# Attention, MLP and experts on one core: load order of the second batch, Silu on ScalarE, and where the early slots' token numbers are cast

## The chip, the core and the metric

One Trainium2 chip, one core of it. The time is that of one execution of the program on the device, in microseconds (us). Engines: TensorE (PE; its weight loads PEld), VectorE (DVE), ScalarE (ACT), GpSimd (POOL), and SyncE (SP), on whose queue nearly all loads and stores are issued, in order.

## The reference

Three stages, each on the output of the one before; the result is out, 2304 x 512.

```python
scores = scale * np.matmul(q, k.transpose(0, 1, 3, 2))          # 4 batches, 8 heads, 576 tokens, 64 wide
ret = np.matmul(scores * Dmat, v)                                # Dmat: causal, gamma[h] ** distance
x = ret.transpose(0, 2, 1, 3).reshape(B * S, H * D)              # 2304 x 512
h = x @ w_in                                                     # 512 -> 2048, w_in and w_out float64
x = ((h * (1.0 / (1.0 + np.exp(-h)))) @ w_out)                   # SiLU, 2048 -> 512
expert_idx = np.argmax(logits, axis=1)                           # logits: cosine of x and 8 expert rows, over tau
for e in range(8):
    mask = expert_idx == e
    out[mask] = gate_w[mask, None] * (np.maximum(x[mask] @ w1[e], 0.0) @ w2[e])
```

## The kernel before

**The MLP** is the frame of the first phase. The 2304 tokens are 6 blocks of 384, and a block takes 16 steps f, one for each 128 columns of w_in. A step has 12 matmuls into h (lines 829 to 831: x and w_in are each split into a high and a low part, xhi, xlo, winh, winl, and three of the four products are formed), then Sigmoid on ScalarE into sg (L834), the multiply of h and sg on VectorE (L835, recorded under the helper's line 137), the split of the result into gh (ScalarE, L843) and gl (POOL), and two steps later 9 matmuls into three y tiles (L857 to 859) with w_out's parts in wo. Steps are counted from 0 over all blocks.

**The weights** come as float64 while block 0 runs. Each of the 32 raw tiles (vraw, 512 KB; 16 of w_in in two DMAs each at L550, 16 of w_out at L547, in the order in which the steps use them) is turned into f32 by a pass on ScalarE (vg, L529) and three on VectorE (L533, L535, L537), then split by a cast on ScalarE (L591) and a subtraction on VectorE (winl or wo, L137). There are four raw buffers: a raw load goes when VectorE has made the last of the three passes on the raw four places earlier. KEPT w_out parts stay as wok; the others are stored in wod and read back as wr for the later blocks. Block 0's end is followed by ent, the expert rows (er), and by yr, the block's rows out of y.

**Attention** is spread under the steps. Batch 0 runs in the startup, batch 1's four head units under block 0, the tails of batches 0 and 1 (the last 192 tokens of each) under block 1, and so on. A head unit transposes q and k, forms three state products (L289), copies and sums them on VectorE (st, st, s: L313 and L137), masks the scores (pt), and in mix forms the rows of x (L264, L275), from which xhi and xlo of the next block are made. Batch 1's loads are 15 DMAs on SP, 256 KB for each third of v, k and q (vn L228, kn L237, qn L212); POOL scales vn and qn once they are in. The tails' kr and qr (L201) are loaded after the last raw; tails need transposes of them (kt, qt, L258).

**Order.** A scheduler places the instructions of each engine by its own model of their times; every engine then runs in that order, and waits for what is not there. issue_after(x) keeps an instruction behind x in the issue order. Batches 2 and 3 are loaded after `anchor`, a late reload of w_out; batch 1 is under no such rule.

**The router** scores the rows of a block against the 8 expert rows on VectorE (jv, L744), ranks the tokens of each expert (rp on TensorE, from oh) and scatters rows into slots (xs) and token numbers with gates into a table (tab). Experts 0 and 1 begin with their first 256 slots, while the last block's steps still run: early_jobs loads the table's part as tke (L974), casts the token numbers to tie (L977) and loads the slots' rows xr (L994). tie is used where an expert's output is scattered to out by POOL (L1150), in the second phase, in which each of the 8 experts goes through 8 steps of two layers; gl of a step is at L1128.

Of the kernel before, what the change touches and what calls it, by code (L numbers as in the profile page):

```python
# [12 lines left out]
AF = mybir.ActivationFunctionType  # L13
ALU = mybir.AluOpType
# [4 lines left out]
I32 = dt.int32  # L19
# [3 lines left out]
B, H, S, HD = 4, 8, 576, 64  # L23
NT, D, F1 = B * S, 512, 2048
E, F2 = 8, 1024
P = 128
KC = D // P
TB = 384
# [71 lines left out]
def body(tc, q, k, v, w_in, w_out, emb, tau, w1, w2, cst, out):  # L100
    nc = tc.nc
# [5 lines left out]
    sub = ALU.subtract  # L107
# [15 lines left out]
    cpool = pool("cpool")  # L123
# [12 lines left out]
    def tt(eng, o, a, b_, op):  # L136
        return eng.tensor_tensor(out=o, in0=a, in1=b_, op=op)  # L137

    def r2f(ap):
        return ap.bitcast(F32)  # L140
# [261 lines left out]
    def side_pv():  # L402
        return ps_v.tile([P, 512], F32, name="pv", tag="pv")

    def after_weights(on):
        return tc.issue_after(anchor[0].ins) if on else nullcontext()

    def prepare(u, psum):

        bt = u.bt  # L410
        if isinstance(u, HeadUnit):
            with after_weights(bt.b >= 2):
                if u.p % 2 == 0 and not bt.rows:
                    bt.load_rows(u.p, u.sg)
                if u.p == 0:
                    for c in range(3):
                        bt.load_chunk(c)
                        if bt.rows:
                            bt.load_queries(c)
            yield 0.05  # L420
        else:
            with tc.issue_after(rawload[0].ins):
                if u.p % 2 == 0:
                    bt.load_rows(u.p, u.sg)
                if u.p == 0:
                    for c in (3, 4):
                        bt.load_chunk(c)
            yield 0.05
        yield from u.prep(psum)
# [110 lines left out]
    def weights():  # L540
# [3 lines left out]
        def load(f, o):  # L544
            r = vpool.tile([P, D, 2], I32, name="vraw", tag="vraw", bufs=RAW)
            if o:
                rawload[0] = nc.sync.dma_start(r.rearrange("p d w -> p (d w)"), w_out32[P * f:P * f + P, :])  # L547
            else:
                for a in range(2):
                    nc.sync.dma_start(r[HD * a:HD * a + HD].rearrange("p (c f) w -> p c (f w)", c=KC),  # L550
                                      w_in32[256 * a:256 * a + 256, 2 * P * f:2 * P * f + 2 * P].rearrange("(c p) f -> p c f", p=HD))
            raw[f, o] = r


# [46 lines left out]
    l2done = [-1]  # L601
    anchor = [None]
    rawload = [None]
    wrload = [None]
    lastw = [None]

# [215 lines left out]
    def first_phase():  # L822
        gq = {}

        def l1(i, f):
            xh, xl = block_x(i)
            h = ps_h.tile([P, 512], F32, name="h", tag="h")
            for c in range(KC):
                nc.tensor.matmul(h[:, :TB], winh[f][:, c], xh[:, c], start=(c == 0), stop=False)  # L829
                nc.tensor.matmul(h[:, :TB], winh[f][:, c], xl[:, c], start=False, stop=False)  # L830
                nc.tensor.matmul(h[:, :TB], winl[f][:, c], xh[:, c], start=False, stop=(c == KC - 1))  # L831
                hook((c + 1) / 8)
            sg = gpool.tile([P, TB], F32, name="sg", tag="sg", bufs=2)
            nc.scalar.activation(sg, h[:, :TB], AF.Sigmoid)  # L834
            tt(nc.vector, sg, h[:, :TB], sg, ALU.mult)  # L835
            return sg

        last = [None]
# [126 lines left out]
    class Slots:  # L965


        def __init__(self, e0, e1, s0, n, m, nm):
            ne = e1 - e0
            self.e0, self.n, self.s0, self.m = e0, n, s0, m  # L970
            rows = tabv[e0:e1, s0:s0 + m]
            self.w = w = m // n
            self.tk = cpool.tile([P, ne, n, 2], F32, name=f"tk{nm}")
            load = nc.sync.dma_start(self.tk[:w].rearrange("p e i c -> p e (i c)"), rows.rearrange("e (p i) c -> p e (i c)", i=n))  # L974
            after_scatters(load, scatters)
            self.ti = cpool.tile([P, ne, n], I32, name=f"ti{nm}")
            nc.vector.tensor_copy(self.ti[:w], self.tk[:w, :, :, 0])  # L977

    class Job:

# [40 lines left out]
        nc.sync.dma_start(jb.raw[n][1], w2[e, n * w:(n + 1) * w].rearrange("(g p) d -> p g d", p=P))  # L1021

    early = []
    ep_ = []
    wp_ = [None]

# [27 lines left out]
    def second_phase():  # L1054
# [57 lines left out]
        def layer1(s):  # L1112
# [12 lines left out]
            gh = gpool.tile([P, TB], F32R, name="gh", tag="gh", bufs=LAG + 1)  # L1125
            gl = gpool.tile([P, TB], F32R, name="gl", tag="gl", bufs=LAG + 1)
            nc.scalar.activation(gh[:, :w], h[:, :w], AF.Relu)  # L1127
            nc.vector.scalar_tensor_tensor(out=gl[:, :w], in0=h[:, :w], scalar=0.0, in1=r2f(gh[:, :w]), op0=ALU.max, op1=sub)  # L1128
            return gh, gl

        def layer2(ss):
# [6 lines left out]
            for j in range(jb.n):  # L1138
# [7 lines left out]
                if f == NF2 - 1:  # L1146
                    e = jb.e - ts.e0
                    ob = gpool.tile([P, D], F32, name="ob", tag="yr", bufs=3)[:ts.w]
                    nc.scalar.activation(ob, y, AF.Copy, scale=ts.tk[:ts.w, e, i, 1:2])  # L1149
                    w = nc.gpsimd.indirect_dma_start(out=out, out_offset=bass.IndirectOffsetOnAxis(ap=ts.ti[:ts.w, e, i:i + 1], axis=0),  # L1150
                                                     in_=ob, in_offset=None, bounds_check=NT - 1, oob_is_err=False)
                    for w0 in puts:
                        tc.declare_no_dep(w.ins, w0.ins.name, reason="no two slots have a token in common")
                    puts.append(w)
# [110 lines left out]
```

## Time and profile before

| | us |
|---|---|
| median of 3 runs | 847.79 |
| lowest, highest | 844.42, 849.81 |
| the profiled execution | 848.8 |
| its span | 847.0 |
| TensorE busy in the span | 798.2 |
| VectorE busy | 538.9 |
| ScalarE busy | 364.9 |
| POOL busy | 263.9 |
| TensorE's idle time for the state sum s, one wait | 5.1 |
| VectorE's idle time for the table tke, one wait | 8.6 |

The span runs from the first to the last instruction of the profiled execution; times below are counted from its start. A busy engine is one that has an instruction running; an idle time is put down to what ended it. The granted clock is TensorE's, as a share of 2.4 GHz: in the records it is at full or at half.

### The profile page before, as it was taken

The numbers are of one execution on the slowest core, as the hardware profiler recorded it, in microseconds if no ns is written. First come the engines' busy times: TensorE is split into PE (matmuls) and PEld (weight loads), VectorE is DVE, ScalarE is ACT, GpSimd is POOL, SyncE is SP. The second block draws the span as 40 slices with busy tenths as digits, with TensorE's granted clock in tenths as the row PEclk, the third lists the DMA queues.
The fourth block names the chain that finished last, engine by engine and source line by source line (L and its number), as shares of the span: only waits on it lengthen the run. The fifth ranks groups of instructions, "written<-read, shape, count | busy, mean of one in ns | idle before, by whom it ended". The sixth has DMA issues, their size and how long they took to land.

```text
span 847.0 us, 13508 instructions
## 1 busy us (share of the span) xinstructions
PE 798.2 (94%) x4638; PEld 667.7 (79%) x4638; DVE 538.9 (64%) x1339; ACT 364.9 (43%) x730; POOL 263.9 (31%) x244
## 2 busy tenths in 40 slices
PE   8787897999999999999999999898999999999994
PEld 5565776777788888888777897787978888888883
DVE  3788896974379528943894389366765555555440
ACT  2454566233342334333423453254655445445341
POOL 3333133355543663364335444202010011011011
PEclk9799999799999999999999999998999999999997
DMA  9978775677622451223302421439478456461000
GB/s 208 214 204 226 195 208 138 161 196 152 98 73 59 107 90 54 44 69 76 81 14 63 125 75 34 104 107 359 107 212 288 127 197 199 124 196 45 2 30 29
DMA packets 164422, 107.78 MB, mean 127 GB/s; under 512 B 100710, under 2 KB 142198, under 8 KB 164352
## 3 DMA queue, kind: packets, MB, share of 16 engines
q1 hardware_dynamic: 160512, 97.42, 44.3%
q0 software_dynamic: 3840, 9.48, 3.0%
q8 instruction: 37, 0.61, 0.3%
q14 instruction: 33, 0.27, 0.1%
HBM read 84.72 MB, written 23.19 MB: 127 GB/s over the span
## 4 chain that ended last, share of the span: by engine, by line
PE 70%; DMA 10%; DVE 9%; issue 4%; SPq 2%; ACT 1%; POOL 1%; POOLq 0%; ACTq 0%; DVEq 0%
PE h L829 7%; PE y L857 6%; PE y L858 6%; PE h L830 6%; PE y L859 6%; PE h L831 6%; DMA vraw<-in_moe_w_out 5%; PE y L1145 4%; PE y L1143 4%; PE y L1144 4%; PE h L1124 4%; PE h L1122 4%; PE h L1123 4%; PE pv L264 3%; DVE jv L744 2%
## 5 line engine op out<-in xcount | busy, mean ns | idle before, releaser
L137 POOL TENSOR_TENSOR gl<-sg,gh 128x384 fp32r<-128x384 f32 x89 | 104.1, 1172 | 191.1 <-ACT gh L843 185.7
L829 PE MATMUL h<-xhi,winh 128*128 128x384 f32 x384 | 136.2, 356 | 5.9 <-ACT winh L591 4.2
L831 PE MATMUL h<-xhi,winl 128*128 128x384 f32 x384 | 132.5, 345 | 3.6 <-DVE winl L137 3.6
L830 PE MATMUL h<-xlo,winh 128*128 128x384 f32 x384 | 132.6, 345 | 0.0
L858 PE MATMUL y<-wo,gh 128*128 128x512 f32 x288 | 114.0, 399 | 3.4 <-DVE wo L137 3.4
L857 PE MATMUL y<-wo,gh 128*128 128x512 f32 x288 | 111.0, 402 | 2.8 <-ACT gh L843 2.8
L859 PE MATMUL y<-wo,gl 128*128 128x512 f32 x288 | 110.6, 398 | 0.3 <-POOL gl L137 0.3
L744 DVE CUSTOM_DVE_ANT_0 jv<-yr,ent 128x512 bf16<-128x512 f32 x120 | 100.8, 840 | 6.0 <-ACT yr L696 5.6
L137 DVE TENSOR_TENSOR sg<-h,sg 128x384 f32<-128x384 f32 x96 | 52.8, 550 | 71.1 <-ACT sg L834 70.8
L843 ACT CAST gh<-sg 128x384 fp32r<-128x384 f32 x96 | 49.1, 512 | 107.2 <-DVE sg L137 105.8
L829 PEld LDWEIGHTS h<-xhi,winh 128*128 128x128 f32 x384 | 73.8, 193 | 18.9 <-ACT winh L591 6.8
L834 ACT ACTIVATE sg<-h 128x384 f32<-128x384 f32 x96 | 47.1, 490 | 94.1 <-PE h L831 88.9
L831 PEld LDWEIGHTS h<-xhi,winl 128*128 128x128 f32 x384 | 73.8, 192 | 5.7 <-DVE winl L137 4.5
L830 PEld LDWEIGHTS h<-xlo,winh 128*128 128x128 f32 x384 | 73.9, 192 | 3.8 <-issue 0.9
L1122 PE MATMUL h<-x2h,h 128*128 128x352 f32 (+1 forms) x236 | 74.9, 317 | 1.5 <-ACT h L1101 1.5
L1143 PE MATMUL y<-h,gh 128*96 128x512 f32 (+1 forms) x190 | 74.5, 392 | 0.4 <-ACT gh L1127 0.4
L1123 PE MATMUL h<-x2l,h 128*128 128x352 f32 (+1 forms) x236 | 74.7, 317 | 0.0
L1145 PE MATMUL y<-h,gl 128*96 128x512 f32 (+1 forms) x190 | 73.7, 402 | 0.0
L1101 ACT CAST h<-w1r 128x512 fp32r<-128x512 f32 x62 | 38.4, 620 | 67.4 <-PE h L1123 59.4
L857 PEld LDWEIGHTS y<-wo,gh 128*128 128x128 f32 x288 | 54.3, 190 | 14.3 <-ACT gh L843 4.1
L1150 POOL DMA_INDIRECT out<-ob,tif x12 | 13.5, 1123 | 165.5 <-ACT ob L1149 163.9
L858 PEld LDWEIGHTS y<-wo,gh 128*128 128x128 f32 x288 | 54.2, 188 | 13.5 <-DVE wo L137 4.6
(636 smaller groups left out, 1566.0 us busy)
## 6 DMA issues: line engine op xcount, KB each, us to landing
w1r<-in_moe_w SPq DMA_DIRECT2D x32, 512.0 KB, 5.8
w2r<-in_moe_w SPq DMA_DIRECT2D x32, 512.0 KB, 5.1
wr<-wod SPq DMA_DIRECT2D x40, 256.0 KB, 2.7
vraw<-in_moe_w_in SPq DMA_DIRECT2D x32, 256.0 KB, 5.7
vraw<-in_moe_w_out SPq DMA_DIRECT2D x16, 512.0 KB, 4.5
xs<-zero SPq DMA_DIRECT2D x11, 512.0 KB, 5.7
yd<-yr SPq DMA_DIRECT2D x18, 256.0 KB, 2.1
vn<-in_v SPq DMA_DIRECT2D x16, 256.0 KB, 3.6
```

What stands on the lines that cost most here:

```text
L137: return eng.tensor_tensor(out=o, in0=a, in1=b_, op=op)
L744: v_.tensor_tensor_reduce(out=jv, in0=rows[j], in1=ent[0][:, e], scale=1.0, scalar=0.0, op0=ALU.mult, op1=ALU.add, accum_out=num[:, j, e:e ...
L829: nc.tensor.matmul(h[:, :TB], winh[f][:, c], xh[:, c], start=(c == 0), stop=False)
L830: nc.tensor.matmul(h[:, :TB], winh[f][:, c], xl[:, c], start=False, stop=False)
L831: nc.tensor.matmul(h[:, :TB], winl[f][:, c], xh[:, c], start=False, stop=(c == KC - 1))
L857: nc.tensor.matmul(y, gh[:, s], w[:, :D], start=(f == 0), stop=False)
L858: nc.tensor.matmul(y, gh[:, s], w[:, D:], start=False, stop=False)
L859: nc.tensor.matmul(y, gl[:, s], w[:, :D], start=False, stop=(f == NF1 - 1))
L1122: nc.tensor.matmul(h[:, :w], h1[:, c], jb.xh[:, c, :w], start=(c == 0), stop=False)
L1123: nc.tensor.matmul(h[:, :w], h1[:, c], jb.xl[:, c, :w], start=False, stop=False)
L1143: nc.tensor.matmul(y, gh[:, sl], h2, start=(f == 0), stop=False)
L1145: m = nc.tensor.matmul(y, gl[:, sl], h2, start=False, stop=(f == NF2 - 1))
```

## The change

Batch 1's loads are put behind rawlast, the last w_in load issued up to that point, which is that of raw 5 (raws counted from 0). Sigmoid and multiply become one activation, Silu. The cast of the token numbers is made where the first scatter needs it, and issued after the last gl before it.

```diff
-    def after_weights(on):
-        return tc.issue_after(anchor[0].ins) if on else nullcontext()
+    def after_weights(b):
+        return tc.issue_after((anchor if b >= 2 else rawlast)[0].ins)
...
         if isinstance(u, HeadUnit):
-            with after_weights(bt.b >= 2):
+            with after_weights(bt.b):
...
                 for a in range(2):
-                    nc.sync.dma_start(r[HD * a:HD * a + HD].rearrange("p (c f) w -> p c (f w)", c=KC),
-                                      w_in32[256 * a:256 * a + 256, 2 * P * f:2 * P * f + 2 * P].rearrange("(c p) f -> p c f", p=HD))
+                    rawlast[0] = nc.sync.dma_start(r[HD * a:HD * a + HD].rearrange("p (c f) w -> p c (f w)", c=KC),
+                                                   w_in32[256 * a:256 * a + 256, 2 * P * f:2 * P * f + 2 * P].rearrange("(c p) f -> p c f", p=HD))
...
+    rawlast = [None]
...
             sg = gpool.tile([P, TB], F32, name="sg", tag="sg", bufs=2)
-            nc.scalar.activation(sg, h[:, :TB], AF.Sigmoid)
-            tt(nc.vector, sg, h[:, :TB], sg, ALU.mult)
+            nc.scalar.activation(sg, h[:, :TB], AF.Silu)
             return sg
...
-            self.ti = cpool.tile([P, ne, n], I32, name=f"ti{nm}")
-            nc.vector.tensor_copy(self.ti[:w], self.tk[:w, :, :, 0])
+            self.nm, self.ti = nm, None
+
+        def tokens(self, e, i):
+
+            if self.ti is None:
+                self.ti = cpool.tile(list(self.tk.shape[:3]), I32, name=f"ti{self.nm}")
+                with tc.issue_after(lastg[0].ins):
+                    nc.vector.tensor_copy(self.ti[:self.w], self.tk[:self.w, :, :, 0])
+            return self.ti[:self.w, e, i:i + 1]
...
+    lastg = [None]
...
-            nc.vector.scalar_tensor_tensor(out=gl[:, :w], in0=h[:, :w], scalar=0.0, in1=r2f(gh[:, :w]), op0=ALU.max, op1=sub)
+            lastg[0] = nc.vector.scalar_tensor_tensor(out=gl[:, :w], in0=h[:, :w], scalar=0.0, in1=r2f(gh[:, :w]), op0=ALU.max, op1=sub)
...
-                    w = nc.gpsimd.indirect_dma_start(out=out, out_offset=bass.IndirectOffsetOnAxis(ap=ts.ti[:ts.w, e, i:i + 1], axis=0),
+                    w = nc.gpsimd.indirect_dma_start(out=out, out_offset=bass.IndirectOffsetOnAxis(ap=ts.tokens(e, i), axis=0),
```

On SP's queue the places of batch 1's loads and of raws 4 and 5 change. Before (vraw of w_out behind batch 1 is raw 4, the next two of w_in are raw 5):

```order
L630 DMA tv<-in_moe_tau 8x1
L228 DMA vn<-in_v 128x8x64
L237 DMA kn<-in_k 128x4x64 x2
L212 DMA qn<-in_q 128x4x64 x2
L228 DMA vn<-in_v 128x8x64
L237 DMA kn<-in_k 128x4x64 x2
L212 DMA qn<-in_q 128x4x64 x4
L237 DMA kn<-in_k 128x4x64 x2
L547 DMA vraw<-in_moe_w_out 128x1024
L228 DMA vn<-in_v 128x8x64
L628 DMA er_430<-in_moe_expert_emb 8x512
L550 DMA vraw<-in_moe_w_in 64x4x256 x2
```

After, from the same place:

```order
L632 DMA tv<-in_moe_tau 8x1
L548 DMA vraw<-in_moe_w_out 128x1024
L630 DMA er_430<-in_moe_expert_emb 8x512
L551 DMA vraw<-in_moe_w_in 64x4x256 x2
L228 DMA vn<-in_v 128x8x64
L237 DMA kn<-in_k 128x4x64 x2
L212 DMA qn<-in_q 128x4x64 x2
L228 DMA vn<-in_v 128x8x64
L237 DMA kn<-in_k 128x4x64 x2
L212 DMA qn<-in_q 128x4x64 x2
L228 DMA vn<-in_v 128x8x64
L237 DMA kn<-in_k 128x4x64 x2
```

Raw 4, the small er and raw 5 now stand ahead of batch 1's 15 loads (the last three of which follow the rows shown); raw 6, of w_out, stands behind them in both.

On VectorE at the start, around the passes on raws 4 and 5. Before:

```order
L537 SCALAR_TENSOR_TENSOR wok_110<-vraw,wok_110 128x512
L535 SCALAR_TENSOR_TENSOR vw<-vg,vw 128x512
L537 SCALAR_TENSOR_TENSOR vw<-vraw,vw 128x512
L137 TENSOR_TENSOR wo<-wok_110,wo 128x512
L137 TENSOR_TENSOR xlo<-pv,xhi 128x2x128
L137 TENSOR_TENSOR winl_120<-vw,winh 128x512
L137 TENSOR_TENSOR xlo<-pv,xhi 128x2x128
L533 TENSOR_SCALAR vw<-vraw 128x512
L535 SCALAR_TENSOR_TENSOR vw<-vg,vw 128x512
L537 SCALAR_TENSOR_TENSOR vw<-vraw,vw 128x512
```

After:

```order
L538 SCALAR_TENSOR_TENSOR wok_110<-vraw,wok_110 128x512
L534 TENSOR_SCALAR vw<-vraw 128x512
L536 SCALAR_TENSOR_TENSOR vw<-vg,vw 128x512
L534 TENSOR_SCALAR vw<-vraw 128x512
L536 SCALAR_TENSOR_TENSOR vw<-vg,vw 128x512
L137 TENSOR_TENSOR wo<-wok_110,wo 128x512
L538 SCALAR_TENSOR_TENSOR vw<-vraw,vw 128x512
L137 TENSOR_TENSOR xlo<-pv,xhi 128x2x128
L536 SCALAR_TENSOR_TENSOR vw<-vg,vw 128x512
L668 TENSOR_SCALAR sq_sce<-ess 8x1
```

The first passes on raws 4 and 5 (vw from vraw) now stand in front of the wo, xlo and winl_120 of the startup; before, that on raw 4 stood behind them, and sg after it.

On VectorE at the change from block 0 to block 1 (st, st, s: state sums of batch 1's last head unit; kt, qt from kr, qr: tails; jv: router of block 0). Before:

```order
L258 STREAM_TRANSPOSE kt<-kr 128x192
L744 ISA jv,num_1700<-yr,ent 128x512
L744 ISA num_1700 128x1
L744 ISA jv,num_1700<-yr,ent 128x512
L744 ISA num_1700 128x1
L313 COPY st<-pv 128x64
L744 ISA jv,num_1700<-yr,ent 128x512
L744 ISA num_1700 128x1
L666 TENSOR_SCALAR sq_scb_1665<-ss 128x3
L137 TENSOR_TENSOR st<-pv,st 128x64
L258 STREAM_TRANSPOSE kt<-kr 128x192
```

After:

```order
L258 STREAM_TRANSPOSE kt<-kr 128x192
L137 TENSOR_TENSOR winl_133<-vw,winh 128x512
L313 COPY st<-pv 128x64
L538 SCALAR_TENSOR_TENSOR wok_117<-vraw,wok_117 128x512
L536 SCALAR_TENSOR_TENSOR vw<-vg,vw 128x512
L137 TENSOR_TENSOR st<-pv,st 128x64
L258 STREAM_TRANSPOSE qt<-qr 128x192
L137 TENSOR_TENSOR wo<-vw,wo 128x512
L258 STREAM_TRANSPOSE kt<-kr 128x192
L538 SCALAR_TENSOR_TENSOR vw<-vraw,vw 128x512
L137 TENSOR_TENSOR s_1213<-pv,st 128x64
```

The state sums stood between the jv products; now they stand among the last weights, behind two kt and one qt of the tails, and the first jv comes later.

On VectorE near the end of the first phase, the cast of the token numbers. Before:

```order
L137 TENSOR_TENSOR sg<-h,sg 128x384
L137 TENSOR_TENSOR gl<-sg,gh 128x384
L977 CAST tie<-tke 128x4
L137 TENSOR_TENSOR wo<-wr,wo 128x512
L137 TENSOR_TENSOR sg<-h,sg 128x384
```

After, it is found in the second phase (l: low parts of the experts' weights):

```order
L1137 SCALAR_TENSOR_TENSOR gl<-h,gh 128x256
L137 TENSOR_TENSOR l__6500<-w2r,h_6499 128x512
L137 TENSOR_TENSOR l__6570<-w1r,h_6569 128x512
L1137 SCALAR_TENSOR_TENSOR gl<-h,gh 128x256
L984 CAST tie<-tke 128x4
L137 TENSOR_TENSOR l__6531<-w2r,h_6530 128x512
```

The cast has moved from in front of a wo of the last block's steps to behind the gl of an expert's step.

## Rows read from the trace of the kernel before

**Rows 1.** The page, first section: busy us of each engine.
```profile
PE 798.2 (94%) x4638; PEld 667.7 (79%) x4638; DVE 538.9 (64%) x1339; ACT 364.9 (43%) x730; POOL 263.9 (31%) x244
```

**Rows 2.** Stretches: length, busy PE, PEld, DVE, ACT, POOL; clock, DMA share, GB/s.
```profile
20.00:42.00 22.00, 16.10 (x116) 11.33 (x114) 16.80 (x33) 10.15 (x20) 7.70 (x6) 0.77 1.10 218
...
42.00:129.00 87.00, 74.63 (x412) 60.28 (x409) 78.26 (x158) 48.18 (x93) 25.97 (x16) 0.98 0.77 206
...
141.00:159.00 18.00, 12.28 (x61) 8.74 (x60) 15.80 (x52) 6.18 (x16) 5.80 (x7) 0.62 0.68 202
...
159.00:515.00 356.00, 356.00 (x2123) 292.96 (x2123) 236.22 (x674) 131.57 (x273) 171.22 (x161) 1.00 0.36 85
...
540.00:550.00 10.00, 6.85 (x26) 5.88 (x26) 4.37 (x9) 2.94 (x6) 0.00 (x0) 0.83 0.37 99
```

**Rows 3.** The chain that ended last, 34 to 47 us: start, length.
```profile
34.98 11.71 DMA vraw<-in_moe_w_out
```

**Rows 4.** Time line of SP: start, length, instruction.
```profile
17.70 0.40 SPq L228 DMA_DIRECT2D vn<-in_v  x1
...
31.62 0.44 SPq L547 DMA_DIRECT2D vraw<-in_moe_w_out  x1
...
32.16 0.38 SPq L228 DMA_DIRECT2D vn<-in_v  x1
...
111.94 4.87 SPq L547 DMA_DIRECT2D vraw<-in_moe_w_out  x2
...
118.33 1.83 SPq L201 DMA_DIRECT2D kr<-in_k  x4
```

**Rows 5.** Time line of VectorE; in brackets the idle time before, and releaser.
```profile
21.79 0.69 DVE L537 SCALAR_TENSOR_TENSOR vw<-vraw,vw 128x512 int32<-128x512 int32 x1
...
24.47 0.68 DVE L537 SCALAR_TENSOR_TENSOR vw<-vraw,vw 128x512 int32<-128x512 int32 x1
...
37.87 0.43 DVE L533 TENSOR_SCALAR vw<-vraw 128x512 int32<-128x512 int32 x1 [1.39 <-DMA vraw<-in_moe_w_out]
...
44.25 0.43 DVE L533 TENSOR_SCALAR vw<-vraw 128x512 int32<-128x512 int32 x1 [1.34 <-DMA vraw<-in_moe_w_in]
...
46.72 0.43 DVE L533 TENSOR_SCALAR wok<-vraw 128x512 int32<-128x512 int32 x1 [0.79 <-DMA vraw<-in_moe_w_out]
```

**Rows 6.** Time line of POOL.
```profile
40.20 1.05 POOL L137 TENSOR_TENSOR vn<-vn,cs 128x512 f32<-128x512 f32 x1 [5.10 <-DMA vn<-in_v]
```

**Rows 7.** Time line of TensorE.
```profile
41.75 0.34 PE L289 MATMUL pv<-vn,kn 128*64 128x64 f32 x4
```

**Rows 8.** Waits from 42 to 129 us: total, times, longest.
```profile
DVE vw L533 <- DMA vraw<-in_moe_w_in: 5.1, 6, 1.3
...
DVE wok L533 <- DMA vraw<-in_moe_w_out: 2.8, 3, 1.0
```

**Rows 9.** Stretch of tile sg: length, busy DVE, ACT, POOL.
```profile
42.00:129.00 87.00, 7.69 (x14) 14.09 (x29) 24.96 (x15) 0.98 0.77 206
```

**Rows 10.** The page, groups of instructions: busy, mean ns.
```profile
L834 ACT ACTIVATE sg<-h 128x384 f32<-128x384 f32 x96 | 47.1, 490 | 94.1 <-PE h L831 88.9
```

**Rows 11.** Time line of VectorE at the change of block.
```profile
141.90 0.69 DVE L744 CUSTOM_DVE_ANT_0 jv<-yr,ent 128x512 bf16<-128x512 f32 x1 [2.96 <-ACT yr L696]
...
146.39 0.21 DVE L137 TENSOR_TENSOR s<-pv,st 128x64 f32<-128x64 f32 x1
```

**Rows 12.** Time line of TensorE there.
```profile
146.75 1.55 PE L264 MATMUL pv<-pt,vn 128*64 128x128 f32 x12 [5.14 <-DVE s L137]
...
158.65 0.34 PE L829 MATMUL h<-xhi,winh 128*128 128x384 f32 x1
```

**Rows 13.** Time line of VectorE at the token numbers.
```profile
542.52 0.17 DVE L977 CAST tie<-tke 128x4 int32<-128x4 f32 x1 [8.63 <-DMA tke<-tab]
```

**Rows 14.** Time line of TensorE there.
```profile
543.33 0.50 PE L858 MATMUL y<-wo,gh 128*128 128x512 f32 x1 [3.15 <-DVE wo L137]
```

**Rows 15.** Time line of TensorE at the router.
```profile
522.70 0.18 PE L764 MATMUL rp<-oh,tri 128*128 128x32 bf16 x1 [1.33 <-DVE oh L137]
```

## The prediction

> **What bounds the kernel now.** I read the page's first section, then the busy time by stretch, then in each stretch with TensorE idle the waits and the time line around it. TensorE is busy 798.2 of 847.0 us [rows 1], so at most 48.8 us of idle time, and what the low clock costs beside it, can go. The stretches show where [rows 2]: from 159 to 515 us TensorE is busy throughout at full clock, and nothing done on another engine there can shorten the program. The losses lie at four places: the startup (20 to 42: 5.9 us idle, granted clock 0.77), the block under which the weights arrive (42 to 129: 12.4 us idle), the change of block (141 to 159: 5.7 us idle, clock 0.62) and the token numbers (540 to 550: 3.2 us idle, clock 0.83). The granted clock moves between two levels, 2.4 and 1.2 GHz, so a mean of 0.62 over 18 us is 2 x 0.38 x 18 = 13.7 us at the lower one.
>
> In 42 to 129 VectorE is the fullest engine, 78.3 of 87 us [rows 2]; its idle 8.7 us are nearly all waits for a raw weight: 5.1 + 2.8 us [rows 8]. Raws come in the order of their use; I count them from 0.
>
> **The change part by part.**
>
> *A, batch 1's loads behind the raws.* In the program before, SP stood in order from 17.70 to 32.5 with batch 1's 15 loads, and raw 4 went at 31.62 [rows 4], though VectorE had read raw 0 for the last time at 21.79 + 0.69 = 22.5 [rows 5]: its buffer was free 9.1 us earlier. VectorE then took raw 4 at 37.87 after a wait of 1.39, raw 5 at 44.25 after 1.34 and raw 6 at 46.72 after 0.79 [rows 5]. In the changed order raws 4 and 5 go as soon as raws 0 and 1 are done (22.5 and, by the row at 24.47, 25.2), and their passes stand in VectorE's order ahead of the last startup pieces. Each raw costs VectorE four passes, 0.43 us for the first and 0.69 for a later one [rows 5], a little less back to back: two raws are some 4.5 us of work, moved into the idle 5.2 us that VectorE has in 20 to 42 (22.00 less 16.80, rows 2). Nothing is removed, so the gain is at most this, or, if it also ends the raw waits up to raw 6, the 9.1 us. On the other side the loads that went at 17.70 now start at about 26 and take the same 15 us, to 41; vn's last chunk was then scaled by POOL at 40.20 [rows 6], and the state products that need it stand in TensorE's order at 41.75 [rows 7]. They were ready just in time; each us that this chunk comes later stops TensorE for one. Bounds: -9.1 to +9 (the 9 us by which their start moves). I take -4, the two raws' passes.
>
> Raw 6 took 11.71 us from issue to VectorE [rows 3], behind batch 1's bytes: it stays behind the same bytes, all of which still have to be moved before it. The Trainium skill ("DMA: Bandwidth & Descriptors", section "Queues, rings and completion order") says that descriptors of one queue start in order on each engine; this trace's 11.71 us agrees. By that rule alone the swap gains nothing beyond raw 5 and A would be near 0, which is the first rival below.
>
> *B, Silu.* 96 multiplies go from VectorE. 14 of them lie in 42 to 129, 7.69 us [rows 9]; most others lie in 159 to 515, where TensorE has no idle time. VectorE falls from 78.3 to 70.6 us there, below TensorE's own 74.6 [rows 2], so that TensorE's 12.4 us of idle time cap A and B together. Silu itself is in no row; the nearest is Sigmoid on the same tile, 490 ns [rows 10]. Twice that would add 14 x 0.49 = 6.9 us to ScalarE, which is busy 48.2 of 87: hidden, so cost 0 from below, and from above at most the same 6.9 us if every one stood on the path. By the Trainium skill ("ScalarE: Activation LUTs", section "What ACT_TABLE_LOAD costs") one element per cycle goes for every function, 186 ns + 0.833 x 384 = 506 ns by estimate, and the sum would not change. The waits for raws (7.9 us) do not go with the multiplies: with four buffers a raw is asked for when the fourth before it is done, and a faster VectorE asks sooner but also stands there sooner. Bounds -7.7 to +6.9; I take -4, half of the multiplies.
>
> *C, the change of block.* VectorE's three small state operations of batch 1's last head unit stood behind the first jv products, and those waited 2.96 us for the evacuated rows, yr; the last of the three, s, ran at 146.39 [rows 11]. TensorE waited 5.14 us for it, began at 146.75 and went at the lower clock until 158.65, where one matmul of h takes 0.34 again [rows 12]. That is 5.7 us idle and some 11.9 us of work at half speed, another 5.9: 11.6 us. Since block 0 now ends with VectorE less full, the three operations stand before the first jv, and the unit's mix inside the y matmuls of step 15. What is late next: in VectorE's new order a kt of the tails stands ahead of winl_133, the last w_in part, and two more transposes ahead of s. They need kr and qr, which SP issues only after the last raw (118.33, over 6 us after 111.94, rows 4). A wait of some us for them holds winl_133, and TensorE's step 15 with it. The stall of 5 us becomes one of perhaps 2, with less time at the lower clock. Bounds -11.6 to +6 (the issue distance just named); I take -6, half.
>
> *D, the token numbers.* The cast waited 8.63 us for its table [rows 13] and held wo<-wr behind it; TensorE waited 3.15 us for that wo [rows 14]. The clock of 0.83 over 10 us is 3.4 us at the lower level, 1.7 us lost. Both go: 4.85. The cast stands now behind ten gl's of the second phase, when the table has long landed; what uses it is POOL's scatter of the first expert's output. What is late next would be the gathered rows xr, which SP asks for behind the table; were TensorE to stand at them, up to the whole comes back. Bounds -4.85 to 0; I take -4.5.
>
> *E, the router of the last block but one.* TensorE waits 1.33 us for oh [rows 15]; VectorE, without the multiplies ahead of it, comes sooner. Bounds -1.3 to 0; I take -0.5.
>
> Sum: -4 -4 -6 -4.5 -0.5 = -19. The profiled execution took 848.8 (span 847.0 and 1.8 around it), so 829.8; the median of the runs shown is 1.0 below that execution. Forecast 829.
>
> **Rivals.**
> 1. *The transfers bind block 0.* A and B are worth nothing: the same bytes stand ahead of raw 6, and a faster VectorE only waits longer for raws. For it: 7.9 of its 8.7 idle us are raw waits, and DMA engines show a share of 1.10 in 20 to 42. Against it: 0.77 in 42 to 129, where there is room. -6 -4.5 -0.5 = -11: 837.
> 2. *The wait at the change of block is only replaced*, by kr and qr for the tails, with the lower clock behind it. For it: the new order on VectorE. C is 0: -13, 835. With rival 1: -5, 843.
> 3. *Batch 1 comes too late (slower).* If raw 5 goes no sooner than before, with 34.98 as the end of its issue [rows 3], batch 1's loads start 17.3 us after 17.70, and vn's last chunk is scaled at about 58 in place of 41. TensorE stands at the state products (ahead of h of the third step), and VectorE at st, ahead of raw 6. 17 us and, as behind the other stall, 5.9 of lower clock in place of A: -15 + 22.9 = +8, 857. It decides from 15 us of delay on (9, if the clock falls too). Against it: the buffers come free at 22.5 and 25.2, and nothing else stands before them on SP.
> 4. *Silu and Tanh do not share a table*, and each of the router's six Tanh calls costs two switches. The Trainium skill ("ScalarE: Activation LUTs", section "Table sets: the hidden batching unit") has one set active at a time. The changed program's ScalarE order shows two table loads in all, as before, and none at Tanh. On ScalarE, half idle, it would take A to E back by little: 831.
>
> **How the numbers follow.** About 1% (8.5 us) is what a measurement of this kernel tells from no change. Forecast 0.56; rival 1 0.14; rival 2 0.13; both together 0.09; rival 3 0.06; rival 4 0.02. The forecast's own range is 820 to 836 (A and B together up to 12.4, C from 0 to -11.6). Faster by over 1%, below 839.3: forecast, rivals 1, 2 and 4, less their upper tails, 0.80. Within 1%: both together and those tails, 0.15. Slower by over 1%: most of rival 3, 0.05. The range leaves out 0.1 on each side: at the bottom all four places give nearly their whole (-12.4 -11.6 -4.85 -1.3 = -30, 818), at the top it takes in both rivals together: 817 to 843.
>
> **What would show it.** Raw 4 and 5 reach VectorE before 33; POOL's last vn of batch 1 at 42 or before; no idle time over 2 us before L289. TensorE's idle time in block 0 falls from 12.4 to about 5, and its first h of block 1 comes some 8 us sooner. At the change of block s runs before jv, and the idle time plus half the time at the lower clock is under 6. No wait for wo near 540. It is wrong if the DMA waits of VectorE in block 0 grow by what the multiplies leave, if kr or qr hold winl_133, or if L289 waits.

## The result and the profile after

The changed kernel took 832.4 us (median of 4 runs, 830.88 to 833.34), the kernel before 847.16 on the same chip: ratio 0.9843, 95% interval 0.9808 to 0.9878. That is 13 us faster by the ratio (10 to 16 by its interval) and 14.8 by the two medians alone; 832.4 lies inside the range of 817 to 843, and 829 was forecast. A second measurement on another chip gave 0.9856 (0.9825 to 0.9888). The profiled execution took 830.88 us, with a span of 828.9 against 847.0.

From the page after, the busy times and the group of Silu (busy us, mean ns of one; idle time before):

```profile
PE 791.5 (95%) x4638; PEld 662.1 (80%) x4638; DVE 496.8 (60%) x1243; ACT 368.2 (44%) x730; POOL 266.9 (32%) x244
...
L836 ACT ACTIVATE sg<-h 128x384 f32<-128x384 f32 x96 | 47.2, 492 | 108.1 <-PE h L833 96.2
```

VectorE is busy 42 us less than in [rows 1]; a Silu takes 492 ns where Sigmoid took 490 [rows 10].

The stretches after, columns as in [rows 2] (the same clock times, so later ones are not the same work):

```profile
20.00:42.00 22.00, 16.41 (x107) 11.32 (x106) 21.25 (x46) 11.54 (x22) 6.53 (x5) 0.69 1.04 210
...
42.00:129.00 87.00, 81.75 (x516) 66.39 (x515) 77.85 (x149) 50.34 (x97) 29.77 (x20) 1.00 0.79 212
...
141.00:159.00 18.00, 15.82 (x81) 11.82 (x81) 17.23 (x46) 8.84 (x20) 10.51 (x9) 1.00 0.76 219
...
159.00:500.00 341.00, 337.35 (x2016) 276.83 (x2015) 192.92 (x588) 129.07 (x262) 167.28 (x156) 1.00 0.35 85
...
540.00:550.00 10.00, 10.00 (x69) 9.13 (x67) 6.89 (x24) 7.78 (x19) 0.00 (x0) 1.00 0.23 81
```

TensorE's idle time in 42 to 129 fell from 12.4 to 5.25 us, and the clock is full at the change of block, where it was 0.62, and near 540, where it was 0.83. From 159 to 500, where there was no idle time before, there are now 3.65 us. From 20 to 42 it is no better: 5.6 us idle, and the clock lower than before, 0.69.

SP after; it answers to [rows 4]:

```profile
22.25 0.37 SPq L548 DMA_DIRECT2D vraw<-in_moe_w_out  x1
...
24.77 1.26 SPq L551 DMA_DIRECT2D vraw<-in_moe_w_in  x2
...
26.07 0.60 SPq L228 DMA_DIRECT2D vn<-in_v  x1
...
33.53 0.55 SPq L228 DMA_DIRECT2D vn<-in_v  x1
...
38.40 0.57 SPq L548 DMA_DIRECT2D vraw<-in_moe_w_out  x1
...
108.15 1.55 SPq L548 DMA_DIRECT2D vraw<-in_moe_w_out  x2
...
111.22 2.21 SPq L201 DMA_DIRECT2D kr<-in_k  x4
```

Raw 4 went at 22.25 in place of 31.62, batch 1's loads from 26.07, and the last raw left SP by 109.7 instead of 116.8. VectorE's first passes on raws 4, 5 and 6, against [rows 5]:

```profile
28.62 0.42 DVE L534 TENSOR_SCALAR vw<-vraw 128x512 int32<-128x512 int32 x1
...
29.82 0.43 DVE L534 TENSOR_SCALAR vw<-vraw 128x512 int32<-128x512 int32 x1 [0.18 <-DMA vraw<-in_moe_w_in]
...
45.99 0.42 DVE L534 TENSOR_SCALAR wok<-vraw 128x512 int32<-128x512 int32 x1
```

Raws 4 and 5 were taken 9 and 14 us sooner. Raw 6 was taken at 45.99, against 46.72, but no longer because of its transfer: SP issued it at 38.40 (the row above), and the trace gives for this one load

```profile
DMA to landing us min/median/max: 4.6/4.6/4.6
```

so it was there at 43.0, where before it landed at 46.7 (34.98 + 11.71, [rows 3]). VectorE was then still busy with what stands ahead of that pass, small operations on the expert rows (er, whose load moved forward too) and the first state sums. VectorE's waits for raws in 42 to 129 were 5.1 and 2.8 us in [rows 8]; after, there is one such row:

```profile
DVE vw L534 <- DMA vraw<-in_moe_w_in: 1.5, 4, 0.5
```

VectorE at the change of block, against [rows 11]:

```profile
118.22 0.38 DVE L258 STREAM_TRANSPOSE kt<-kr 128x192 f32<-128x192 f32 x1 [1.97 <-DMA kr<-in_k]
...
123.05 0.21 DVE L137 TENSOR_TENSOR s<-pv,st 128x64 f32<-128x64 f32 x1
...
141.50 1.17 DVE L746 CUSTOM_DVE_ANT_0 jv<-yr,ent 128x512 bf16<-128x512 f32 x1 [2.55 <-ACT yr L698]
```

A kt of the tails waited 1.97 us for kr, as was feared; s ran at 123.05, long before the first jv. TensorE's longest wait there is now 1.66 us, for the rows' evacuation (yr), against 5.14 in [rows 12]:

```profile
141.52 0.50 PE L858 MATMUL y<-wo,gh 128*128 128x512 f32 x1 [1.66 <-ACT yr L698]
```

### The profile page after: what moved, and what is told of

Read it like the earlier page. It is cut to its first block, busy times and chain, and to the rows that moved or that the text cites. A ratio compares the mean times of both kernels' runs of the same rounds, so it can differ in the third digit from the quotient of the medians.

```text
span 828.9 us, 13425 instructions
## 1 busy us (share of the span) xinstructions
PE 791.5 (95%) x4638; PEld 662.1 (80%) x4638; DVE 496.8 (60%) x1243; ACT 368.2 (44%) x730; POOL 266.9 (32%) x244
## 4 chain that ended last, share of the span: by engine, by line
PE 66%; DVE 12%; DMA 8%; issue 5%; SPq 4%; ACT 3%; POOL 0%; DVEq 0%; POOLq 0%; ACTq 0%
PE h L831 6%; PE y L858 6%; PE y L859 6%; PE y L860 6%; PE h L832 6%; PE h L833 5%; PE y L1152 4%; PE y L1154 4%; PE y L1153 4%; DVE jv L746 4%; PE h L1133 4%; PE h L1131 4%; PE h L1132 4%; DMA vraw<-in_moe_w_in 3%; PE pv L264 2%
## 5 line engine op out<-in xcount | busy, mean ns | idle before, releaser
L137 POOL TENSOR_TENSOR gl<-sg,gh 128x384 fp32r<-128x384 f32 x89 | 107.4, 1210 | 155.3 <-ACT gh L844 133.7
L831 PE MATMUL h<-xhi,winh 128*128 128x384 f32 x384 | 134.1, 350 | 3.0 <-ACT xhi L513 1.7
L832 PE MATMUL h<-xlo,winh 128*128 128x384 f32 x384 | 130.8, 341 | 0.0
L860 PE MATMUL y<-wo,gl 128*128 128x512 f32 x288 | 112.9, 396 | 1.8 <-POOL gl L137 1.8
L746 DVE CUSTOM_DVE_ANT_0 jv<-yr,ent 128x512 bf16<-128x512 f32 x120 | 91.2, 760 | 7.4 <-ACT yr L698 7.1
L137 DVE TENSOR_TENSOR wo<-wok,wo 128x512 fp32r<-128x512 f32 x48 | 39.4, 820 | 71.7 <-ACT wo L620 71.6
L860 PEld LDWEIGHTS y<-wo,gl 128*128 128x128 f32 x288 | 53.9, 188 | 13.6 <-POOL gl L137 2.7
```

What stands on the lines that cost most here:

```text
L746: v_.tensor_tensor_reduce(out=jv, in0=rows[j], in1=ent[0][:, e], scale=1.0, scalar=0.0, op0=ALU.mult, op1=ALU.add, accum_out=num[:, j, e:e ...
L860: nc.tensor.matmul(y, gl[:, s], w[:, :D], start=False, stop=(f == NF1 - 1))
```

## The experiments

Twelve kernels ran, each against runs of the kernel before on the same chip. Because some stages repeat from one profiled execution to another far better than the whole (steps 84 to 95 took 48.28 us in both profiled executions of the change, whose spans are 828.9 and 839.7), the table also gives, from the profiled executions, the start of step 0's and the time between steps' activations of h (sg on ScalarE's time line): steps 0 to 24 hold block 0 and the change of block, steps 84 to 95 the router's end and the token numbers. Steps 0 to 24 repeat less well: 138.12 and 140.27 for the change, 137.75 and 142.53 for loads_only and loads_tie, which differ only in the later cast. Nor is the profiled execution always a typical one: it lies 7.5 us above the median of its runs in whole, 5.1 above in loads_tie, 4.4 above in silu_tie, and 3.7 below in loads_only.

| kernel | ratio to before (95% interval) | sg of step 0 | steps 0 to 24 | steps 84 to 95 |
|---|---|---|---|---|
| before | 1 | 40.40 | 150.92 | 53.44 |
| tie_only | 0.9972 (0.9945 to 1.0) | 39.20 | 149.90 | 48.42 |
| jv_pin | 0.9977 (0.9951 to 1.0002) | 39.41 | 145.58 | 52.60 |
| silu_block0 | 0.9962 (0.9937 to 0.9987) | 40.23 | 144.40 | 53.17 |
| silu_only | 0.9884 (0.9843 to 0.9926) | 39.77 | 141.87 | 48.49 |
| silu_tie | 0.9893 (0.9857 to 0.993) | 44.97 | 141.97 | 48.29 |
| loads_only | 0.9925 (0.9893 to 0.9957) | 41.53 | 137.75 | 50.48 |
| loads_tie | 0.9833 (0.9803 to 0.9863) | 42.03 | 142.53 | 48.41 |
| loads_silu | 0.9876 (0.9839 to 0.9914) | 42.24 | 140.13 | 48.52 |
| the change | 0.9843 (0.9808 to 0.9878) | 41.34 | 138.12 | 48.28 |
| whole (again) | 0.9856 (0.9825 to 0.9888) | 50.61 | 140.27 | 48.28 |
| passes_late | 0.9863 (0.9822 to 0.9904) | 43.23 | 136.46 | 48.25 |
| batch1_later | 0.9865 (0.9825 to 0.9906) | 42.97 | 137.07 | 48.28 |
| raw5_late | 0.9857 (0.982 to 0.9893) | 43.80 | 140.75 | 48.25 |

**One part alone.** The diff of the change cut to one of its three parts: loads_only has after_weights and rawlast, silu_only Silu, tie_only tokens() and lastg.

Expected of loads_only: 

> Only the order of batch 1's loads is changed; Sigmoid, multiply and the early cast stay as before. In this kernel's order too the three state sums of batch 1's last head unit stand ahead of the first jv. Theory 1 (the prediction's parts: loads -4, change of block -6): -10 us against before. Theory 2 (the gain in block 0 is that of the multiplies alone, the loads only swap places): -6 from the change of block, and TensorE's idle time from 42 to 129 us stays within 2 us of before's 12.4. Theory 3 (the change of block is bound by kr and qr, not by the place of the sums): 0 to -4.

Expected of silu_only: 

> Only Silu; loads and cast as before. Its order has the state sums ahead of jv as well. Theory 1: -4 in block 0 and -6 at the change of block, -10. Theory 2: TensorE's idle time from 42 to 129 falls by 7 or more, and the total is -13 to -14. If Silu does nothing under the weights (the transfers bind): -6.

Expected of tie_only: 

> Only the cast of the token numbers moves. All theories: -4.5 (bounds -3 to -5), TensorE's wait of 3.15 us for wo near 540 gone, and the clock at full there; everything before 520 us as in the kernel before within 1 us. If the rows xr take the place of the table as the last to come: 0 to -1.

By the ratios (of 847 us) the loads alone are worth 6.4 us, Silu 9.8, the cast 2.4: 18.6 together, where the change gives 12 to 13. This excess is no larger than what the intervals leave open together (about 6 us, by estimate), so the stages have to show whether the parts overlap. Theory 1's 10 us came out for Silu, not for the loads (3.6 to 9.1 us by the interval), and the cast's gain (0 to 4.7) leaves open whether the forecast 4.5 is right. The waits of VectorE for raws in 42 to 129 show two different reliefs. With the loads alone:

```profile
DVE vw L534 <- DMA vraw<-in_moe_w_in: 1.4, 3, 0.8
```

with Silu alone:

```profile
DVE vw L533 <- DMA vraw<-in_moe_w_in: 6.8, 8, 1.9
```

So the loads' order takes most of the raw waits away (7.9 to 1.4 us; 4.2 in the profiled execution of loads_tie, with the same order of loads) and leaves the multiplies; Silu takes the multiplies away and leaves the waits (6.8 here and 0.2 for w_out). TensorE's idle time in that stretch was 5.8 us with the loads alone and 9.3 with Silu alone, so theory 2, by which the loads only swap places, falls. And near 540, with Silu alone and the cast still early, VectorE waits as long as ever for the table (first row), while TensorE is busy all the time (second row, the stretch):

```profile
530.04 0.17 DVE L976 CAST tie<-tke 128x4 int32<-128x4 f32 x1 [7.99 <-DMA tke<-tab]
```

```profile
515.00:545.00 30.00, 30.00 (x148) 26.55 (x147) 13.30 (x26) 14.37 (x27) 6.37 (x6) 1.00 0.32 80
```

VectorE has less to do between its subtractions into wo (13.30 us of the 30) and stands far enough ahead for the wait not to be felt. With the loads alone the wait for wo remained, smaller than in [rows 14]:

```profile
529.87 0.50 PE L860 MATMUL y<-wo,gh 128*128 128x512 f32 x1 [1.80 <-DVE wo L137]
```

**Two parts.**

Expected of silu_tie: 

> The whole change without the order of the loads. Theory 1: -14.5. Theory 2: the loads are worth nothing, so this equals the changed kernel within 2 us, -15 to -18, and its first steps come as early or earlier. A theory by which the loads carry block 0 expects -10.5.

Expected of loads_silu: 

> The change without the late cast. Theory 1 (the parts add): 4.5 us less gain than the whole change, so -9 against before, with TensorE waiting 3 us for wo behind the cast. Theory 4 (the parts overlap: with Silu VectorE stands so far ahead that its wait for the table no longer reaches TensorE): as the whole change, within 2 us, -12 to -14; VectorE still waits 6 to 8 us for tke, and TensorE has no idle time there.

Expected of loads_tie: 

> The change without Silu. Theory 1: -4 -6 -4.5 = -14.5. Theory 4: the loads' -6 and a cast that was worth only what TensorE still waited for wo beside the loads alone (1.8 us and some lower clock): -8 to -9; TensorE's idle time from 42 to 129 us stays above 8 us, since the multiplies are still there.

Expected of whole: 

> The changed kernel again, on the same chip as the three others, as their measure: -13 to -15 against before. Theory 1 has it 4.5 us faster than the change without the late cast, theory 4 within 2 us of it.

With Silu in place the late cast gains nothing measurable (silu_tie against silu_only, 0.9893 and 0.9884; the change against loads_silu, 0.9856 and 0.9876 on one chip), and steps 84 to 95 take 48.3 to 48.5 us with either or both: theory 4. silu_tie's 9 us (5.9 to 12.1) lie by the theory for which the loads carry block 0 (10.5), below theories 1 and 2. The change without Silu (loads_tie, 0.9833) is as fast as the change. It was expected 8 to 9 us faster than before, or 14.5 if the parts added; it gained 14 (11.6 to 16.7), the number of theory 1, and more than its parts alone (6.4 and 2.4) by about as much as the intervals leave open. Its stages show no such surplus (steps 0 to 24: 142.53), but its profiled execution was the slowest of its seven runs. So for the loads with the cast an overlap is not shown.

**The change of block alone.** The kernel before, with this edit:

```diff
-            tt(nc.vector, s3, ps[:, 2], s[:, 1], ALU.add)
+            sums[bt.b] = tt(nc.vector, s3, ps[:, 2], s[:, 1], ALU.add)
...
+                with tc.issue_after(sums[1].ins) if i == 0 else nullcontext():
                     v_.tensor_tensor_reduce(out=jv, in0=rows[j], in1=ent[0][:, e], scale=1.0, scalar=0.0,
```

Expected: 

> The kernel before, with the first block's jv products kept behind the last state sum of batch 1 and nothing else: the order of VectorE at the change of block, alone. If the stall there came from the sums standing behind jv's wait for yr (theory 1): TensorE's 5.14 us wait for s goes, the clock stays at full from 141 to 159, -5 to -6. If kr, qr or the expert rows take its place (rival 2): 0 to -2, with a new wait of 3 us or more between 141 and 159.

VectorE ran s at 137.66, before the first jv, and TensorE's wait for it is gone; but the next in line show on TensorE, xhi and a place behind the router's small operations (sq_tb):

```profile
137.66 0.22 DVE L137 TENSOR_TENSOR s<-pv,st 128x64 f32<-128x64 f32 x1
...
138.91 0.69 DVE L746 CUSTOM_DVE_ANT_0 jv<-yr,ent 128x512 bf16<-128x512 f32 x1 [1.03 <-DMA qr<-in_q]
```

```profile
141.96 0.62 PE L831 MATMUL h<-xhi,winh 128*128 128x384 f32 x2 [1.59 <-ACT xhi L282]
...
144.66 1.42 PE L363 MATMUL ps<-qt,kt 64*128 64x192 f32 x8 [2.08 <-DVE sq_tb L137]
```

Two waits of 1.59 and 2.08 us stand in place of 5.14, and the clock over 141 to 159 is 0.81 instead of 0.62. Steps 0 to 24 are 5.3 us shorter than before (4.3 shorter than in tie_only, whose order is that of before there); the ratio shows 2 us, with 0 inside its interval. Theory 1 and rival 2 each hold in part: the place of the sums was the stall, and 3.67 us of other waits (0.58 of them for xhi were there before) stand in place of its 5.14, with less time at the lower clock.

**Silu in block 0 alone.**

```diff
-            nc.scalar.activation(sg, h[:, :TB], AF.Sigmoid)
-            tt(nc.vector, sg, h[:, :TB], sg, ALU.mult)
+            nc.scalar.activation(sg, h[:, :TB], AF.Silu if i == 0 else AF.Sigmoid)
+            if not (i == 0):
+                tt(nc.vector, sg, h[:, :TB], sg, ALU.mult)
```

Expected: 

> The kernel before with Silu in block 0 alone; blocks 1 to 5 keep Sigmoid and the multiply. Theory 4 (Silu's gain is block 0 with the change of block, and in the last block the cover for the cast's wait; between them nothing): the first 24 steps as with Silu everywhere (9 us less than before), the wait for wo near 540 is back as in the kernel before, so 4 to 5 us slower than Silu everywhere: -5 to -6. If the multiplies in the other blocks cost something: -2 or less. Theory 1 with its parts: -10.

The wait for wo is back:

```profile
536.37 0.51 PE L859 MATMUL y<-wo,gh 128*128 128x512 f32 x1 [2.89 <-DVE wo L137]
```

Steps 0 to 24 gained 6.5 us of the 9 that Silu everywhere gave, steps 84 to 95 nothing, and the ratio is 0.9962, 3 us where 5 to 6 were expected. The difference from silu_only in steps 84 to 95 (53.17 against 48.49) is 4.7 us, as theory 4 has it; its first 24 steps were to gain the whole 9.

**The startup.** In all kernels with the new order of the loads step 0's sg came at 41.3 or later; without it at 39.2 to 40.4 (silu_tie's 44.97 apart, see the last section). Two tries asked why. passes_late is the change with VectorE's first pass on raws 4 and 5 behind the startup's last xlo:

```diff
+        with tc.issue_after(lastlo[0].ins) if 4 <= n <= 5 else nullcontext():
             nc.vector.tensor_scalar(o, raw[:, :, 0], 29, None, op0=ALU.logical_shift_right)
```

Expected: 

> The whole change, with VectorE's passes on raws 4 and 5 kept behind the last xlo of the startup; their loads go as early as in the change. Theory 5 (the early passes delay the startup: with the new order of the loads the first h comes some 1.5 us later, and that is the passes standing ahead of xlo and winl): the first sg 1.5 us earlier than in the changed kernel, the time 1 to 2 us shorter, -14 to -16. Theory 6 (the gain of the loads is the passes' work moved into the startup): the gain shrinks by up to 4 us, to -9 to -10. If both hold they cancel: as the whole change.

Step 0 came no sooner (43.23), so theory 5 finds no support, though ScalarE's wait ahead of xhi, shown below, was 1.1 us longer here. Steps 0 to 24 did not lengthen (136.46), as theory 6 would have had them do; but the passes, held back from 28.6 to 37.9, were still done by 41.2, ahead of step 0's activation, so theory 6 is not settled by this. ScalarE's time line shows what delayed the start. In the change (first fence) and in passes_late (second), vg of raw 5 waits for its transfer, and the startup's xhi stands behind it:

```profile
29.78 0.67 ACT L530 ACTIVATE vg<-vraw 128x512 f32<-128x512 f32 x1 [3.34 <-DMA vraw<-in_moe_w_in]
...
30.86 0.36 ACT L513 CAST xhi<-pv 128x256 fp32r<-128x256 f32 x1
```

```profile
30.99 0.66 ACT L530 ACTIVATE vg<-vraw 128x512 f32<-128x512 f32 x1 [4.44 <-DMA vraw<-in_moe_w_in]
...
32.06 0.37 ACT L513 CAST xhi<-pv 128x256 fp32r<-128x256 f32 x1
```

TensorE in the change waits 1.73 us for that xhi (before, 1.14 by the same row), which begins its first h. In the other kernels with the new order of the loads this wait is 1.64 to 3.28 us (raw5_late apart), without it 0.47 to 0.65:

```profile
31.28 1.01 PE L831 MATMUL h<-xhi,winh 128*128 128x384 f32 x2 [1.73 <-ACT xhi L513]
```

raw5_late therefore puts both passes behind that xhi and its xlo:

```diff
+                with tc.issue_after(his[-2].ins) if n + 1 == 5 else nullcontext():
                     rebias(raw[order[n + 1]], gi[n + 1])
...
+        with tc.issue_after(los[-2].ins) if n == 5 else nullcontext():
             nc.vector.tensor_scalar(o, raw[:, :, 0], 29, None, op0=ALU.logical_shift_right)
```

Expected: 

> The whole change, with ScalarE's pass on raw 5 behind the startup's second xhi from the end, and VectorE's first pass on it behind the xlo that goes with that. Theory 7 (the loads' order delays the startup by ScalarE's pass on raw 5: it waits 3.3 us for the transfer, in order ahead of that xhi, and TensorE with it): TensorE's wait for xhi at the first h falls from 1.73 us to 1 or less, the first sg comes at 39.5 to 40.5 in place of 41.3 and later, the time 1 to 2.5 us shorter than the changed kernel's, 828 to 832 on its chips, ratio to before 0.981 to 0.984. If something else holds the startup (the lower clock, VectorE): first sg at 41 or later, ratio as the change's, 0.984 to 0.986.

The wait fell to 1.15, what it was before:

```profile
33.75 1.01 PE L834 MATMUL h<-xhi,winh 128*128 128x384 f32 x2 [1.15 <-ACT xhi L513]
```

but the ratio is that of the change, 0.9857, where 0.981 to 0.984 was expected of theory 7, and this execution's startup ran at the lower clock from about 9 to 19 us already, so its 43.80 says nothing. The wait is shown; that it is worth time is not.

**More raws ahead.** batch1_later is the change with two more raws ahead of batch 1's loads:

```diff
-        while ready[0] < 0:
+        while ready[0] < 2:
             next(wg)
```

Expected: 

> The whole change with batch 1's loads behind raws 6 and 7 as well (the weights' generator is run two raws further before the loads are placed); in TensorE's order half of the first state products then stand behind h of step 3. If earlier raws are what the loads' order gives (the prediction's A): raw 6 reaches VectorE some 10 us sooner, idle time in 42 to 129 falls further, -15 to -17. If it is used up after two raws: as the whole change, -12 to -14. Rival 3 (batch 1 too late): TensorE waits for vn or kn at L289 or at the first transposes for some 5 to 10 us, -4 to -8.

0.9865, as the change: VectorE took raw 6 at 34.02, 12 us sooner, and TensorE's idle time in 42 to 129 is 4.95 us, against 5.25. Two raws ahead use up the gain. TensorE waited 0.76 us for vn at L289, no more, since the scheduler moved half of the state products to the step after. No version beat the change beyond its interval.

## Why the prediction was right, and where its sum failed

The direction, the range and three of the four places were right; the startup gained nothing. The sum of 19 was 4 us too large by the medians and 6 by the ratio. No stall stands twice in it: it is the single parts of the experiments that share stalls (C is in the loads and in Silu, D in Silu and in the cast), and their 18.6 us are close to 19 by chance. Where the terms went is shown by the stages. These are steps 0 to 24 and steps 84 to 95, before and after each (columns as in [rows 2]):

```profile
40.40:191.32 150.92, 132.83 (x773) 105.41 (x774) 127.01 (x307) 74.54 (x148) 51.57 (x41) 0.94 0.71 190
41.34:179.46 138.12, 127.36 (x773) 101.23 (x774) 117.68 (x269) 72.23 (x143) 52.56 (x41) 1.00 0.77 208
...
499.97:553.41 53.44, 48.70 (x237) 42.84 (x236) 37.97 (x108) 17.20 (x36) 15.31 (x14) 0.97 0.25 60
489.18:537.46 48.28, 46.71 (x236) 41.53 (x235) 32.12 (x90) 18.21 (x35) 18.54 (x15) 1.00 0.24 66
```

D and E were forecast at 5 and came to 5.2. A, B and C were forecast at 14 and came to 12.8 in this pair, 7.3 of it idle time of TensorE and 5.5 busy time (as many instructions, 773, at a mean clock of 1.00 in place of 0.94); by the other executions of these orders (149.90 in tie_only; 140.13 and 140.27 in loads_silu and whole) it is as little as 9.6. Two losses stand against this that the sum put at nothing. Step 0 came 0.9 us later in this pair, and 1.1 to 1.8 later in loads_only, loads_tie and loads_silu. And between steps 24 and 84, where TensorE had no idle time before, every kernel with Silu in all blocks has 1.0 to 1.1 us of it; in the change this is one wait:

```profile
422.50 0.76 PE L264 MATMUL pv<-pt,vn 128*64 128x192 f32 x3 [1.05 <-DVE pt L137]
```

Together this is 12 to 16 us, as the ratio and the medians have it. What follows step 95 is left out; it varies from 289 to 294 us over all the kernels, and nothing was forecast there. So A was too large by its startup, and C by the idle time that stayed.

- *A.* The loads went as worked out, and POOL was done with vn's last chunk at 41 us, as before. The raw waits went, not the startup's idle time: the loads bring 13.2 us in steps 0 to 24 alone and 8.4 with the late cast, the change of block included, but the start came about 1 to 2 us later. I counted VectorE's passes on raws 4 and 5 and not ScalarE's, which waits for the raw in order ahead of xhi. That the gain is the two raws' passes moved into the idle time of 20 to 42 is not shown: raw 4's first pass lay there before already (37.87, [rows 5]), and passes_late, which held the passes back, lost nothing. That A and B together came near their 8 is luck in part.
- *B.* "The waits for raws (7.9 us) do not go with the multiplies" held for Silu alone (7.9 to 7.0 us). Silu alone brought 9 us in steps 0 to 24, with the change of block in it; beside the loads it adds little that one execution each can show (137.75 and 142.53 without Silu; 140.13, 138.12 and 140.27 with it). A and B were forecast at 8 together; TensorE's idle time in 42 to 129 fell by 7.1, with 5.25 left where about 5 were named.
- *C.* The place of the sums, yr's wait and the kr row came as worked out. Both edits move the sums ahead of jv, each by itself (the order of loads_only and of silu_only has it), so C is in both single results. Alone it was 4 to 5 us in the stage, against 6. But that the stall of 5 us becomes one of perhaps 2 holds for the longest wait only. From step 14 to step 24, before and after, TensorE's idle time is 5.72 and 6.13 us, in the change in several waits of at most 1.66; what went there is the lower clock:

```profile
124.93:191.32 66.39, 60.67 (x371) 47.25 (x370) 51.98 (x154) 26.39 (x56) 27.00 (x27) 0.90 0.61 165
117.36:179.46 62.10, 55.97 (x318) 42.77 (x318) 48.12 (x136) 25.40 (x54) 28.19 (x27) 1.00 0.68 184
```

- *D.* 4.5 forecast, 5.0 in the stage with the cast alone (53.44 to 48.42). In the change the cast's new place was worth nothing beside Silu, which frees this stall by itself. I had valued it as if the multiplies still stood behind the cast.
- *E.* The wait for oh is gone in the change, but a wait for wo of 1.29 us stands at 501; nothing gained.
- *Rivals.* Rival 1 fell with the raw waits: the transfers did not bind. What the Trainium skill ("DMA: Bandwidth & Descriptors", section "Queues, rings and completion order") says of descriptors starting in order agrees with the trace: raw 6, still issued behind batch 1's loads, landed at 43.0, after the last of these whose landing the trace has, a kn at 40.24. But that raw 6 would come no sooner did not follow: it landed 3.7 us sooner than before, and VectorE took it as late only because of its own order. The raws in front of these bytes carried the gain; batch1_later, with raw 6 ahead of them too, gained no more. Rival 2 was half right (jv_pin, and the idle time under C), rival 3 did not occur, even with two more raws ahead. Of rival 4: the change has two table loads, as before. The 492 ns of Silu lie under the estimate of 506 from the Trainium skill ("ScalarE: Activation LUTs", section "What ACT_TABLE_LOAD costs").

Open stays why the change without Silu is no slower than with it, as its one profiled execution is the slowest of its runs, and why the ratio shows less than half of what tie_only and jv_pin gain in their stages (5.0 and 5.3 us; the intervals reach 4.7 and 4.2). The profiled execution of the kernel before, 848.8, lies 1 to 4 us above the medians of before in these measurements; single executions of one kernel differ by 5 us and more, and one profile for each cannot settle it.

## What to carry to other kernels

Before adding the gains of several edits, ask of each stall which of the edits removes it: here the cast's new place gained nothing once Silu had taken the multiplies from VectorE, though the wait for the table was as long as ever. After a stall is removed, add up the idle time of the whole stage and not only the longest wait. A load that is issued earlier brings its consumers forward on every engine that takes it in order; look at the smallest of them, here one pass of 0.67 us on ScalarE, for what stands behind it. Kernels with one part each, and with one part missing, cost little and show both.

## What was not expected of the hardware

The clock in the startup differs between executions of the same order. The change's profile shows, by 5 us (columns as in [rows 2]):

```profile
10.00:15.00 5.00, 4.87 (x50) 3.66 (x48) 2.74 (x9) 1.07 (x3) 2.12 (x3) 1.00 1.29 218
...
20.00:25.00 5.00, 4.29 (x46) 2.71 (x44) 4.78 (x13) 4.06 (x8) 0.00 (x0) 1.00 0.87 207
```

and the same kernel in the execution profiled as "whole":

```profile
10.00:15.00 5.00, 5.00 (x31) 3.75 (x31) 1.54 (x5) 0.55 (x1) 2.14 (x3) 0.50 1.30 216
...
20.00:25.00 5.00, 5.00 (x31) 3.75 (x30) 1.94 (x5) 0.71 (x2) 0.00 (x0) 0.50 0.53 107
...
50.00:55.00 5.00, 5.00 (x36) 4.28 (x35) 4.45 (x21) 1.56 (x4) 2.01 (x2) 1.00 1.02 277
```

TensorE is at least as busy in the second, and from about 9 us on the second runs at 1.2 GHz instead of 2.4, to nearly 50 us; its step 0 comes 9.3 us later, and its span is 839.7 instead of 828.9. silu_tie and raw5_late show 0.50 from 10 to 15 and full clock again from 20. All of them did the same work up to about 9 us. What decides it was not found. The profiled executions of whole and silu_tie, which show it, lie 7.5 and 4.4 us above the medians of their runs, that of raw5_late 0.5 below: it seems a part of the spread of the runs, and is a reason to read gains from the stages and not from two spans.

Also not expected: Silu and Sigmoid do not share a table here. With Silu in block 0 and Sigmoid after it the trace has three table loads of 1283 ns in place of two, while Tanh needs none beside either.
